# Attention and two gated layers on one core: the order of parking, reloading and forming token sums around the turn from pass one to pass two

## The chip, the cores and the metric

One core of one Trainium2 chip runs the kernel. The metric is device time in microseconds of one launch. Before the change the median of three runs is 987.12 us (986.42 to 987.84).

## The reference

The inputs are attention tensors for 4 batches of 8 heads, 512 local and 32 global positions of 64 numbers each, and the weights of two layers. After the attention there are 4 * 544 = 2176 tokens of 512 numbers (2048 local, 128 global).

```python
s_ll = where(|i - j| <= 32, scale * q_l @ k_l.T, -1e9)     # local rows see a band and the global keys
out_l = softmax([scale * q_l @ k_g.T, s_ll]) @ [v_g, v_l]
out_g = softmax(scale * q_g @ [k_g, k_l].T) @ [v_g, v_l]
x = [out_g, out_l]                                          # (2176, 512)
y = (sigmoid(x @ w_gate) * (x @ w_val)) @ w_out             # 512 -> 1536 -> 512: the gated layer
h = y @ w_in                                                # 512 -> 2048
P = a0 + a1*h + a2*h^2 + a3*h^3
Q = 1 + |b0|*|h| + |b1|*h^2
out = (P / (Q + 1e-6)) @ w_out2                             # 2048 -> 512: the rational layer
```

The change touches the gated layer and the edge to the rational one. The attention is untouched.

## The kernel before

Everything that TensorE multiplies is held as a high and a low part, and a product is three matmuls (high by high, high by low, low by high). Tokens stand in five tiles: 0 to 3 with 512 tokens each, and tile 4, the 128 global rows. `xh`/`xl` are the layer's inputs, `yh`/`yl` its outputs; they share buffers by tag (`xh0` is tile 0's high part, and so on).

**Gated layer, pass one** (line 861, six blocks of two features of 128). A block does for tile 0 `first` of both features (each 12 matmuls into `pg`, 12 into `pv`, then gate, high and low part), `first_glob` for the global rows (turned: tokens on the output's partitions), the two halves of `second` for tile 0, then `turn`, which transposes the gated global rows into `pt`, `first` of both features for tile 1, and `second_glob`. The halves of `second` for tile 1 are left pending and run in the next block, behind its first `first`. `second` adds into `acc` in SBUF (`gacc`). PSUM has two pools: ps1 with three banks (`pg`, `pv`, `pgv`, `pt`, `pty`, and `pa`, `pb`, `pc`) and ps2 with five (results of the second products).

**Weights beside it** (class `Weights`, line 450). A raw float64 weight tile is fetched and split by steps: `magnitude` (two passes on ScalarE, into a `v` tile and a `q` tile), `bits` (three on VectorE, which also asks for the raw tile three further on), `add` (GpSimd), `hi` (ScalarE), `lo` (GpSimd). For the features of pass two the gate and value tiles are also combined in four steps (`combine`, line 625) into the weights of a seven-product scheme. What is finished is stored to device memory (`keep`, line 594) and loaded back later (`pump`, line 647), in the order of `loads`, each as soon as its place in SBUF is free. `AT_ONCE` (line 458) says how many tiles of the second layer are split in each block. `Pace` (line 685) puts the steps into the instruction order: each step has a cost, `advance(dt)` is called after each piece of TensorE work, and emits steps until their summed cost has the share of the total that the time so far has of the block's 34.0.

Each engine runs its instructions in the order written here. SP's queue (SyncE) issues all DMAs, in order too: a DMA that waits holds those behind it.

**End of pass one.** The last block (features 10 and 11) makes the final sums. For tiles 0 and 1 their high and low parts are made at once in a `st` tile (three buffers, shared with the weights) and stored (lines 843 to 848): they are *parked*, since their SBUF places are needed for pass two. `final_glob` (line 804) transposes the finished global rows at the end of the block.

**Pass two** is for tiles 2 and 3. Features 0 and 1 go the plain way in the *opening* (lines 1044 to 1069). Between its pieces `combos` forms the token sums (`za` to `ze`, steps c1 to c4 for k = 0 and 1) and copies them as high and low parts (`put`) into `turned`, which lies where tiles 0 and 1 were. Features 2 to 11 go through `strassen` (line 952): seven products `g0, s2, s1, g1, s3, v1, s4` of six matmuls on three banks, with up to two pending halves of `second` put between them (after `g1` and after `s3`). At the end, line 1080, the parked tiles 0 and 1 are loaded back, and `rational` begins with tile 0.

Of the kernel before, what the change touches and what calls it, by code (L numbers as in the profile page):

```python
# [449 lines left out]
class Weights:  # L450
# [7 lines left out]
    AT_ONCE = (0, 1, 1, 1, 1, 8)  # L458
    RING2 = (4, 5, 6, 7, 0, 1, 2, 3, 8, 9, 10, 11)

    def __init__(self, tc, early, dram, ins, outs):
# [14 lines left out]
        for p, f in enumerate(range(2, NF + 1, 2)):  # L476
# [3 lines left out]
            else:  # L480
# [8 lines left out]
        self.plan = [[(0.1, step, j) for step, j in ((self.magnitude, a), (self.magnitude, b), (self.bits, a), (self.add, a),  # L489
                      (self.bits, b), (self.add, b), (self.hi, a), (self.lo, a), (self.hi, b), (self.lo, b))]]  # L490
        self.urgent, self.plan = self.plan[0], []
# [21 lines left out]
        self.loaded = 0  # L513
# [42 lines left out]
    def magnitude(self, j):  # L556
# [89 lines left out]

    def pump(self, last):

        while self.loaded < last:
# [82 lines left out]
def gated(nc, pools, only, xpool, dram, wp, ident, xh, xl):  # L732
# [48 lines left out]
    def turn(f0, t):  # L781

        ps = pools.ps1.tile([128, 512], F32, tag="p1", name=f"pt{f0}")
# [32 lines left out]
    parked = {}  # L816

    def second(f0, i, gs, half):
# [17 lines left out]
        for m in ms:  # L836
            a = acc[i][:, m]
            if f0 == 0:
                nc.vector.tensor_copy(a, ps[m])
            else:  # L840
                nc.vector.tensor_tensor(a, ps[m], a, ALU.add)  # L841
            if final:
                t = wp.stage(f"y{i}{m}") if i < 2 else None
                h, l = (yh[i][:, m], yl[i][:, m]) if i > 1 else (t[:, 0:512], t[:, 512:1024])
                nc.scalar.copy(h, a)
                (nc.vector if m % 2 else nc.gpsimd).tensor_tensor(l, a, h.bitcast(F32), ALU.subtract)
                if i < 2:
                    wp.keep((9, i, "y", m), t)
        if half == 1 and i in (1, 3):
# [8 lines left out]
    for _, step, j in wp.urgent:  # L858
        step(j)
    pending = []  # L860
    for p, f0 in enumerate(range(0, NF, G)):
        pace = Pace(wp.plan[p], 34.0)
        gs = [first(f0, 0)]
        pace.advance(2 * L)
        for half in pending:
            half()
            pace.advance(L)
        gs.append(first(f0 + 1, 0))
        pending = pair_of(f0, 0, gs)
        pace.advance(2 * L)  # L870
        t = first_glob(f0)
        pace.advance(3)
        for half in pending:
            half()
            pace.advance(L)
        gg = turn(f0, t)
        gs = [first(f0, 1)]
        pace.advance(2 * L)
# [15 lines left out]
    turned = []  # L894

    def combos():

        names = ("xh0", "xl0", "xh1", "xl1")
        t12h, t12l, t34h, t34l = (xpool.tile([128, 4, 512], F32R, tag=n, name=f"t{n}") for n in names)
        turned.extend([(t12h[:, 0:2], t12l[:, 0:2]), (t12h[:, 2:4], t12l[:, 2:4]),  # L900
                       (t34h[:, 0:2], t34l[:, 0:2]), (t34h[:, 2:4], t34l[:, 2:4])])
        part = {(r, c): (xh[2 + c][:, 2 * r : 2 * r + 2].bitcast(F32), xl[2 + c][:, 2 * r : 2 * r + 2].bitcast(F32))
                for r in range(2) for c in range(2)}

        def tile(name):
            return only.tile([128, 512], F32, tag="z", name=name, bufs=6)

        def put(i, k, src, eng):
            h, l = (t[:, k] for t in turned[i])
            nc.scalar.copy(h, src)  # L910
            eng.tensor_tensor(l, src, h.bitcast(F32), ALU.subtract)

        held = {}

        def less(dst, x, y, eng):

            for d, a, b in zip(dst, x, y):
                eng.tensor_tensor(d, a, b, ALU.subtract)
            eng.tensor_tensor(dst[0], dst[0], dst[1], ALU.add)

        def at(rc, k):
            return [t[:, k] for t in part[rc]]

        def c1(k):
            held["a", k], held["b", k] = tile(f"za{k}"), tile(f"zb{k}")
            less((held["a", k], held["b", k]), at((0, 1), k), at((0, 0), k), nc.vector)

        def c2(k):
            h, l = at((1, 1), k)
            a, b = held["a", k], held["b", k]  # L930
            nc.gpsimd.tensor_tensor(b, h, a, ALU.subtract)
            nc.gpsimd.tensor_tensor(b, b, l, ALU.add)

        def c4(k):
            h, l = at((1, 0), k)
            b = held["b", k]
            c = held["c", k] = tile(f"zc{k}")
            nc.vector.tensor_tensor(c, h, b, ALU.subtract)
            nc.vector.tensor_tensor(c, c, l, ALU.add)

        def c3(k):
            held["d", k], held["e", k] = tile(f"zd{k}"), tile(f"ze{k}")
            less((held["d", k], held["e", k]), at((1, 1), k), at((0, 1), k), nc.gpsimd)

        out = []
# [423 lines left out]
```

## Time and profile before

| what | us |
|---|---|
| median of three runs | 987.12 |
| the profiled execution | 990.42 |
| its span, first to last instruction | 988.2 |
| TensorE busy in it | 920.2 (93%) |
| VectorE busy | 743.1 (75%) |
| ScalarE busy | 581.3 (59%) |
| GpSimd busy | 570.8 (58%) |

In the profile PE is TensorE, DVE VectorE, ACT ScalarE, POOL GpSimd, and SP the queue that issues DMAs. L709 is line 709 of the kernel, and `pg<-xh,w10gv` names what an instruction writes and reads. Times are microseconds from the start of the span. "Idle before, releaser" says what an engine waited for. PEclk is the TensorE clock that was granted in a stretch, 1.00 being full. A line inside a helper stands for all of its callers, so tile names tell more. The mean granted clock of the whole span is 0.965.

### The profile page before, as it was taken

How to read it: one execution, taken by the hardware profiler on the slowest of the kernel's cores; microseconds unless marked ns; L12 is line 12 of the kernel's file. 1: busy time of each engine (PE TensorE's matmuls, PEld its weight loads, DVE VectorE, ACT ScalarE, POOL GpSimd, SP SyncE). 2: the span in 40 equal slices, each digit the busy share in tenths (PEclk: the TensorE clock that was granted, in tenths of full speed). 3: DMA queues.
4: the chain of work that ended last, by engine and by line, in shares of the span. 5: the costliest groups of instructions: out<-in, count | busy, mean ns of one | idle time of the engine just before them, and what ended most of it. 6: DMA issues, size and time to landing. Idle time of an engine off the chain costs nothing.

```text
span 988.2 us, 13773 instructions
## 1 busy us (share of the span) xinstructions
PE 920.2 (93%) x4666; PEld 756.2 (77%) x4666; DVE 743.1 (75%) x1355; ACT 581.3 (59%) x1161; POOL 570.8 (58%) x470
## 2 busy tenths in 40 slices
PE   8989999798989979768999969899999999999998
PEld 6878877687878757557888857788888888888886
DVE  6988965866768665785666655987778889888887
ACT  6979854444444443333433435777777778777773
POOL 4766755656556553564565552644456567566654
PEclk9999999999989989789999989999999999999999
DMA  8754365656656786449788774000300220020112
GB/s 301 231 193 137 88 243 193 232 194 213 224 203 216 246 305 213 181 136 404 253 293 297 265 263 179 10 1 24 126 22 0 86 86 1 1 86 1 43 54 86
DMA packets 60805, 156.24 MB, mean 158 GB/s; under 512 B 7104, under 2 KB 9152, under 8 KB 60736
## 3 DMA queue, kind: packets, MB, share of 16 engines
q1 hardware_dynamic: 60640, 155.24, 45.1%
q8 instruction: 37, 0.61, 0.3%
q14 instruction: 32, 0.26, 0.1%
q10 hardware_dynamic: 96, 0.13, 0.1%
HBM read 103.17 MB, written 52.17 MB: 157 GB/s over the span
## 4 chain that ended last, share of the span: by engine, by line
PE 69%; DVE 10%; POOL 6%; DMA 5%; ACT 5%; issue 4%; SPq 1%; POOLq 0%; DVEq 0%; ACTq 0%
PE rp L1220 6%; PE rp L1218 6%; PE rp L1219 6%; PE rp L710 5%; PE rp L711 5%; PE rp L709 5%; PE p L828 2%; PE p L829 2%; PE p L827 2%; PE pair L261 2%; PE pg L709 2%; PE pg L710 2%; PE pg L711 2%; PE pb L959 1%; PE bank L380 1%
## 5 line engine op out<-in xcount | busy, mean ns | idle before, releaser
L1135 POOL TENSOR_TENSOR v<-v,u 128x512 f32<-128x512 f32 x68 | 90.8, 1336 | 120.5 <-ACT v L1131 120.5
L1189 POOL TENSOR_TENSOR rgl<-t,rgh 128x512 fp32r<-128x512 f32 x64 | 90.0, 1406 | 40.6 <-POOL v L1135 18.9
L1143 DVE TENSOR_TENSOR t<-rp,t 128x512 f32<-128x512 f32 x68 | 46.8, 688 | 54.8 <-ACT t L1139 53.7
L1128 ACT ACTIVATE u<-rp 128x512 f32<-128x512 f32 x68 | 40.5, 596 | 73.6 <-PE rp L711 70.0
L295 POOL TENSOR_TENSOR p<-p,r 128x448 f32<-128x448 f32 x64 | 58.6, 940 | 36.3 <-DVE r L290 23.3
L1164 DVE SCALAR_TENSOR_TENSOR v<-v,u 128x512 f32<-128x512 f32 x68 | 74.7, 1099 | 0.0
L1168 DVE SCALAR_TENSOR_TENSOR t<-t,co,v 128x512 f32<-128x512 f32 x68 | 72.9, 1072 | 2.4
L280 ACT ACTIVATE p<-p,mx 128x224 f32<-128x224 f32 x128 | 60.4, 484 | 8.0 <-DVE mx L272 8.0
L841 DVE TENSOR_TENSOR gacc<-p,gacc 128x512 f32<-128x512 f32 x80 | 52.2, 684 | 14.2 <-PE p L829 14.2
L1160 DVE SCALAR_TENSOR_TENSOR v<-v,u 128x512 f32<-128x512 f32 x68 | 59.1, 869 | 1.1 <-ACT u L1156 1.1
L1131 ACT ACTIVATE v<-u,co 128x512 f32<-128x512 f32 x68 | 55.6, 817 | 2.3
L755 ACT CAST gh<-t 128x512 fp32r<-128x512 f32 x38 | 23.5, 618 | 55.2 <-DVE t L748 50.3
L1152 ACT ACTIVATE u<-v,co 128x512 f32<-128x512 f32 x68 | 49.2, 724 | 6.7 <-POOL v L1135 6.7
L1139 ACT ACTIVATE t<-rp,co 128x512 f32<-128x512 f32 x68 | 51.8, 761 | 0.5 <-POOL rgl L1189 0.5
L760 DVE TENSOR_TENSOR gl<-t,gh 128x512 fp32r<-128x512 f32 x38 | 31.9, 840 | 24.6 <-ACT gh L755 24.6
L1147 DVE SCALAR_TENSOR_TENSOR t<-t,co,rp 128x512 f32<-128x512 f32 x68 | 50.2, 738 | 0.0
L1156 ACT ACTIVATE u<-u,co 128x512 f32<-128x512 f32 x68 | 48.5, 713 | 2.3 <-DVE t L1143 2.2
L1177 ACT CAST rgh<-t 128x512 fp32r<-128x512 f32 x64 | 39.0, 610 | 15.4 <-DVE t L1168 15.4
L272 DVE CUSTOM_DVE_ANT_0 p<-pair,masks 128x224 f32<-128x224 f32 x128 | 42.2, 384 | 7.4 <-PE pair L261 6.2
L748 DVE TENSOR_TENSOR t<-pv,t 128x512 f32<-128x512 f32 x28 | 19.3, 688 | 33.9 <-PE pv L711 22.3
L1243 POOL TENSOR_TENSOR racc<-ev,racc 128x512 f32<-128x512 f32 x22 | 37.9, 1744 | 0.0
L709 PE MATMUL rp<-yh,w20in 128*128 128x512 f32 x64 | 26.1, 408 | 9.1 <-issue 9.1
(1388 smaller groups left out, 3215.9 us busy)
## 6 DMA issues: line engine op xcount, KB each, us to landing
raw1gv<-in_w_gate_val SPq DMA_DIRECT2D x24, 512.0 KB, 3.5
raw2in<-in_w_in SPq DMA_DIRECT2D x16, 512.0 KB, 4.3
raw2out<-in_w_out SPq DMA_DIRECT2D x16, 512.0 KB, 3.9
kn<-in_k_l SPq DMA_DIRECT2D x15, 448.0 KB, 5.5
raw1out<-in_w_out SPq DMA_DIRECT2D x12, 512.0 KB, 3.7
vn<-in_v_l SPq DMA_DIRECT2D x16, 256.0 KB, 4.0
out<-racc SPq DMA_DIRECT2D x16, 256.0 KB, 2.0
qn<-in_q_l SPq DMA_DIRECT2D x15, 256.0 KB, 4.7
```

The source lines that it names most:

```text
L280: nc.scalar.activation(p, p, AF.Exp, bias=s["mx", half][:, n : n + 1], scale=-1.0, accum_out=s["sm", half][:, n, 0:1])
L709: nc.tensor.matmul(ps, wh, mh[:, k], start=k == 0, stop=False)
L710: nc.tensor.matmul(ps, wh, ml[:, k], start=False, stop=False)
L711: nc.tensor.matmul(ps, wl, mh[:, k], start=False, stop=k == 3)
L1135: nc.gpsimd.tensor_tensor(s["v"], s["v"], s["u"], ALU.mult)
L1160: nc.vector.scalar_tensor_tensor(s["v"], s["v"], Q_CONST, s["u"], ALU.add, ALU.mult)
L1164: nc.vector.scalar_tensor_tensor(s["v"], s["v"], 2.0, s["u"], ALU.subtract, ALU.mult)
L1168: nc.vector.scalar_tensor_tensor(s["t1"], s["t1"], a0, s["v"], ALU.add, ALU.mult)
L1189: nc.gpsimd.tensor_tensor(s["gl"], s["t1"], s["gh"].bitcast(F32), ALU.subtract)
L1218: nc.tensor.matmul(ps, gh[:, w], wh, start=k == 0, stop=False)
L1219: nc.tensor.matmul(ps, gh[:, w], wl, start=False, stop=False)
L1220: nc.tensor.matmul(ps, gl[:, w], wh, start=False, stop=k == G - 1)
```

## The change

Seven things, all in the order of work or in buffers:

- `AT_ONCE` goes from (0, 1, 1, 1, 1, 8) to (0, 2, 2, 2, 2, 5): blocks 1 to 4 split one more tile of the second layer each, the last block three fewer. The summed cost of a middle block's steps goes from 29.3 to 32.8.
- Buffers: ring `z` (combined weights, token sums, temporaries of the products) six to five, ring `q` two to three.
- `turn` takes its bank from ps2, not from ps1.
- The parked results of tiles 0 and 1 are no longer made at once: tile 0's four go to the last two spots of the last block, tile 1's four one by one into the opening.
- In the last block and the opening, loads are asked for one by one (`allow(1)`), at spots listed by hand.
- The token sums c1, c2, c4 and c3 of k = 0 run in the last block, those of k = 1 and all `put` in the opening, in a written order; no weight is split in the opening, and the rest has a pace of 143.0 over the products (174.0 over both before). `final_glob` moves behind the opening's first `first`. In block 0 the last four of the early steps move behind its first `first`.
- The parked tile 0 is asked back in feature 11 behind the product `s1`, tile 1 behind `v1`.

```diff
-    AT_ONCE = (0, 1, 1, 1, 1, 8)
+    AT_ONCE = (0, 2, 2, 2, 2, 5)
...
-            v = self.only.tile([128, 512], U32, tag="z", name=f"v{name}", bufs=6)
+            v = self.only.tile([128, 512], U32, tag="z", name=f"v{name}", bufs=5)
...
-        q = self.early.tile([128, 512], U32, tag="q", name=f"q{name}", bufs=2)
+        q = self.early.tile([128, 512], U32, tag="q", name=f"q{name}", bufs=3)
...
+    def allow(self, n):
+        self.limit += n
+        self.pump(self.limit)
...
-        while self.loaded < last:
+        while self.loaded < min(last, len(self.loads)):
...
-        ps = pools.ps1.tile([128, 512], F32, tag="p1", name=f"pt{f0}")
+        ps = pools.ps2.tile([128, 512], F32, tag="p2", name=f"pt{f0}")
...
             if final:
-                t = wp.stage(f"y{i}{m}") if i < 2 else None
-                h, l = (yh[i][:, m], yl[i][:, m]) if i > 1 else (t[:, 0:512], t[:, 512:1024])
-                nc.scalar.copy(h, a)
-                (nc.vector if m % 2 else nc.gpsimd).tensor_tensor(l, a, h.bitcast(F32), ALU.subtract)
-                if i < 2:
+                def park(h, l, m=m):
+                    nc.scalar.copy(h, acc[i][:, m])
+                    (nc.vector if m % 2 else nc.gpsimd).tensor_tensor(l, acc[i][:, m], h.bitcast(F32), ALU.subtract)
+
+                def away(m=m, park=park):
+                    t = wp.stage(f"y{i}{m}")
+                    park(t[:, 0:512], t[:, 512:1024])
                     wp.keep((9, i, "y", m), t)
+
+                if i > 1:
+                    park(yh[i][:, m], yl[i][:, m])
+                else:
+                    parks.append(away)
...
+        extra = {}
+        if f0 + G == NF:
+            load = lambda: wp.allow(1)
+            extra = {0: [load], 1: [load], 2: [lambda: c1(0)], 3: [load], 4: [load, lambda: c2(0)], 5: [load, lambda: c4(0)],
+                     6: [load], 7: [lambda: c3(0)] + [lambda: parks.pop(0)()] * 2, 8: [lambda: parks.pop(0)()] * 2}
+        spots = iter(range(9))
+
+        def spot(dt):
+            pace.advance(dt)
+            for step in extra.get(next(spots), []):
+                step()
+
         gs = [first(f0, 0)]
-        pace.advance(2 * L)
+        if p == 0:
+            for step, j in wp.urgent[6:]:
+                step(j)
+        spot(2 * L)
...
-        if f0 + G == NF:
-            final_glob()
...
+        spot(0)
         pace.finish()
-        if f0 + 2 * G >= NF:
-            wp.pump(len(wp.loads))
...
+    def back(i):
+        yh[i] = xpool.tile([128, 4, 512], F32R, tag=f"xh{i}", name=f"yh{i}")
+        yl[i] = xpool.tile([128, 4, 512], F32R, tag=f"xl{i}", name=f"yl{i}")
+        for m in range(4):
+            t = wp.kept[9, i, "y", m]
+            nc.sync.dma_start(yh[i][:, m].bitcast(F32), t[:, 0:512])
+            nc.sync.dma_start(yl[i][:, m].bitcast(F32), t[:, 512:1024])
...
         late(2)
+        if f == NF - 1:
+            back(0)
         product(a, "g1", x[1, 0], False)
...
         product(b, "v1", turned[3], False)
+        if f == NF - 1:
+            back(1)
...
     gs = [first(0, 2)]
-    some(2)
-    pace.advance(2 * L)
-    for half in pending:
-        half()
-        some(1)
-        pace.advance(L)
-    wp.pump(len(wp.loads))
+    final_glob()
+    put(0, 0, "a", nc.vector)
+    put(1, 0, "b", nc.vector)
+    wp.allow(1)
+    pending.pop(0)()
+    put(3, 0, "c", nc.gpsimd)
+    park()
+    pending.pop(0)()
+    put(2, 0, "d", nc.vector)
+    park()
+    wp.allow(1)
     gs.append(first(1, 2))
...
-    wp.pump(len(wp.loads))
+    wp.allow(len(wp.loads))
+    pace = Pace(actions, 143.0)
```

The rest of the opening goes on in the same way: c1(1), park, c2(1), a load; behind `first(0, 3)` put, park, c4(1), a load; the two halves with two puts, c3(1) and a load; behind `first(1, 3)` the last put.

## Rows read from the trace of the kernel before

**Rows 1.** Who makes PE wait, whole span: us in total, times, longest us

```profile
PE pg L709 <- ACT t L747: 18.6, 5, 6.5
PE rp L709 <- issue: 9.1, 1, 9.1
PE pv L709 <- ACT t L747: 8.5, 2, 7.0
PE pb L959 <- ACT t L747: 7.4, 1, 7.4
...
PE pb L959 <- DVE w L974: 3.5, 2, 2.7
```

**Rows 2.** Busy time by stretch: length, then busy us (instructions) per engine, clock, DMA

```profile
core 0: us, PE busy (x) PEld busy (x) DVE busy (x) ACT busy (x) POOL busy (x), PEclk, DMA share, GB/s
124.63:159.71 35.08, 32.44 (x155) 26.65 (x154) 22.75 (x40) 18.74 (x34) 19.61 (x18) 1.00 0.65 233
159.71:331.85 172.14, 158.81 (x705) 130.47 (x704) 120.11 (x187) 78.19 (x142) 103.86 (x83) 0.94 0.60 209
331.85:381.17 49.32, 41.17 (x182) 33.17 (x180) 31.77 (x47) 22.03 (x39) 24.75 (x19) 0.90 0.77 277
381.17:423.73 42.56, 35.52 (x147) 28.81 (x145) 31.01 (x38) 13.94 (x25) 23.28 (x17) 0.88 0.48 179
423.73:463.20 39.47, 28.55 (x109) 22.29 (x108) 27.24 (x35) 15.37 (x28) 22.65 (x17) 0.88 0.74 276
583.97:600.00 16.03, 6.86 (x20) 4.34 (x20) 2.12 (x5) 4.59 (x8) 3.33 (x3) 0.68 1.03 373
...
423.74:584.50 160.76, 149.25 (x637) 121.26 (x635) 107.22 (x158) 61.19 (x109) 91.53 (x71) 0.97 0.78 275
```

**Rows 3.** PE in order of time, block 4: starts of three `pg` layers

```profile
290.17 0.39 PE L709 MATMUL pg<-xh,w18gv 128*128 128x512 f32 x1
...
301.05 0.39 PE L709 MATMUL pg<-xh,w19gv 128*128 128x512 f32 x1
...
314.97 0.48 PE L709 MATMUL pg<-xh,w18gv 128*128 128x512 f32 x1
```

**Rows 4.** ACT in order of time, block 4, in front of the late sigmoid

```profile
321.80 0.67 ACT L567 ACTIVATE q110out<-raw1out 128x512 uint32<-128x512 uint32 x1 [2.48 <-POOL v111gv L583]
...
322.63 0.61 ACT L747 ACTIVATE t<-pg 128x512 f32<-128x512 f32 x1
```

**Rows 5.** Who makes ACT wait, 331.85 to 463.20

```profile
ACT v26out L566 <- POOL st24in L613: 7.4, 1, 7.4
...
ACT sty L845 <- DMA k91y<-sty: 5.3, 2, 4.7
...
ACT sty L845 <- DMA k90y<-sty: 3.7, 2, 3.0
```

**Rows 6.** DVE and POOL in order of time: a weight's steps, gate, combining, sums

```profile
291.67 0.42 DVE L574 TENSOR_SCALAR v18out<-v18out 128x512 f32<-128x512 f32 x1
...
292.58 0.69 DVE L576 SCALAR_TENSOR_TENSOR v18out<-raw1out,v18out 128x512 uint32<-128x512 uint32 x1
...
311.52 0.42 DVE L748 TENSOR_TENSOR t_glob<-pgv,t_glob 128x256 f32<-128x256 f32 x1
...
311.68 1.29 POOL L583 TENSOR_TENSOR v111gv<-v111gv,q111gv 128x512 uint32<-128x512 uint32 x1 [1.09 <-DVE v111gv L576]
...
315.52 0.43 DVE L634 TENSOR_TENSOR v110gv<-v110gv,v110gv 128x256 f32<-128x256 f32 x1 [0.84 <-POOL v110gv L632]
...
388.99 0.69 DVE L918 TENSOR_TENSOR za<-xh,xh 128x512 f32<-128x512 f32 x1
...
404.54 1.75 DVE L938 TENSOR_TENSOR zc<-xh,zb 128x512 f32<-128x512 f32 x1
```

**Rows 7.** SP's queue at the end of pass two, and how long these loads took

```profile
574.37 0.32 SPq L658 DMA_DIRECT2D w21out<-k21out  x1
...
585.75 0.61 SPq L1085 DMA_DIRECT2D yh<-k90y  x1
...
yh<-k90y SPq DMA_DIRECT2D x4, 256.0 KB, 7.2
```

More of the change, by code (lines that the diff above doesn't have):

```diff
@@ L512, in __init__ @@
         self.two = {key: self.RING2[n % 12] for n, key in enumerate(two)}
-        self.loaded = 0
+        self.loaded = self.limit = 0
         self.places, self.free = {}, [True] * 12
@@ L814, in final_glob @@
         nc.vector.tensor_tensor(yl[GLOB], src, yh[GLOB].bitcast(F32), ALU.subtract)
-    parked = {}
+    parks = []
     def second(f0, i, gs, half):
@@ L854, in pair_of, with ztile, put, less @@
         return [lambda h=h: second(f0, i, gs, h) for h in range(2)]
-    for _, step, j in wp.urgent:
+    turned, held = [], {}
+    part = {(r, c): (xh[2 + c][:, 2 * r : 2 * r + 2].bitcast(F32), xl[2 + c][:, 2 * r : 2 * r + 2].bitcast(F32))
+            for r in range(2) for c in range(2)}
+    def ztile(name):
+        return only.tile([128, 512], F32, tag="z", name=name, bufs=5)
+    def put(i, k, x, eng):
+        if not turned:
+            t12h, t12l, t34h, t34l = (xpool.tile([128, 4, 512], F32R, tag=n, name=f"t{n}") for n in ("xh0", "xl0", "xh1", "xl1"))
+            turned.extend([(t12h[:, 0:2], t12l[:, 0:2]), (t12h[:, 2:4], t12l[:, 2:4]),
+                           (t34h[:, 0:2], t34l[:, 0:2]), (t34h[:, 2:4], t34l[:, 2:4])])
+        src = held[x, k]
+        h, l = (t[:, k] for t in turned[i])
+        nc.scalar.copy(h, src)
+        eng.tensor_tensor(l, src, h.bitcast(F32), ALU.subtract)
+    def less(dst, x, y, eng):
+        for d, a, b in zip(dst, x, y):
+            eng.tensor_tensor(d, a, b, ALU.subtract)
+        eng.tensor_tensor(dst[0], dst[0], dst[1], ALU.add)
+    def at(rc, k):
+        return [t[:, k] for t in part[rc]]
+    def c1(k):
+        held["a", k], held["b", k] = ztile(f"za{k}"), ztile(f"zb{k}")
+        less((held["a", k], held["b", k]), at((0, 1), k), at((0, 0), k), nc.vector)
+    def c2(k):
+        h, l = at((1, 1), k)
+        a, b = held["a", k], held["b", k]
+        nc.gpsimd.tensor_tensor(b, h, a, ALU.subtract)
+        nc.gpsimd.tensor_tensor(b, b, l, ALU.add)
+    def c4(k):
+        h, l = at((1, 0), k)
+        b = held["b", k]
+        c = held["c", k] = ztile(f"zc{k}")
+        nc.vector.tensor_tensor(c, h, b, ALU.subtract)
+        nc.vector.tensor_tensor(c, c, l, ALU.add)
+    def c3(k):
+        held["d", k], held["e", k] = ztile(f"zd{k}"), ztile(f"ze{k}")
+        less((held["d", k], held["e", k]), at((1, 1), k), at((0, 1), k), nc.gpsimd)
+    for step, j in wp.urgent[:6]:
         step(j)
@@ L886, in gated @@
                 wp.release((1, f0 + g, "gv", h))
+        spot(0)
         pace.finish()
-        if f0 + 2 * G >= NF:
-            wp.pump(len(wp.loads))
     actions = list(wp.plan[-1])
[L894 to L945, printed above, removed]
-        for k in range(2):
-            out += [lambda k=k: c1(k), lambda k=k: c2(k), lambda k=k: put(0, k, held["a", k], nc.vector),
-                    lambda k=k: c4(k), lambda k=k: put(1, k, held["b", k], nc.vector), lambda k=k: c3(k),
-                    lambda k=k: put(3, k, held["c", k], nc.gpsimd), lambda k=k: put(2, k, held["d", k], nc.vector)]
-        return out
@@ L970, in tile @@
         def tile(name):
-            return only.tile([128, 512], F32, tag="z", name=f"{name}{f}", bufs=6)
+            return only.tile([128, 512], F32, tag="z", name=f"{name}{f}", bufs=5)
         def add(out, ps, t):
@@ L1034, in strassen, with park @@
         return [l0, l1, l2, l3]
-    t_steps = combos()
-    pace = Pace(actions, 174.0)
-    def some(n):
-        for _ in range(n):
-            if t_steps:
-                t_steps.pop(0)()
-    gs = [first(0, 2)]
-    some(2)
-    pace.advance(2 * L)
-    for half in pending:
-        half()
-        some(1)
-        pace.advance(L)
-    wp.pump(len(wp.loads))
+    def park():
+        if parks:
+            parks.pop(0)()
+    gs = [first(0, 2)]
+    final_glob()
[9 more added lines that the diff above has]
+    wp.allow(1)
     gs.append(first(1, 2))
-    some(3)
-    pace.advance(2 * L)
+    c1(1)
+    park()
+    c2(1)
+    wp.allow(1)
     pending = pair_of(0, 2, gs)
     gs = [first(0, 3)]
-    some(3)
-    pace.advance(2 * L)
-    for half in pending:
-        half()
-        some(2)
-        pace.advance(L)
+    put(0, 1, "a", nc.vector)
+    park()
+    c4(1)
+    wp.allow(1)
+    pending.pop(0)()
+    put(1, 1, "b", nc.vector)
+    c3(1)
+    pending.pop(0)()
+    put(3, 1, "c", nc.gpsimd)
+    wp.allow(1)
     gs.append(first(1, 3))
-    some(16)
-    pace.advance(2 * L)
+    put(2, 1, "d", nc.vector)
     for f in range(G):
```

29 lines of the change are left out of this document (13 added, 16 removed).

## The prediction

> **What bounds the kernel now.** I first asked who makes TensorE (PE) wait [rows 1], because the page shows PE busy for 93% of the span and no other engine above 75%. In the two passes of the gated layer PE lost time at few places. It waited 18.6 us in five pieces before the first matmul of `pg` (6.5 us the longest), 8.5 us before `pv`, 7.4 us and 3.5 us before `pb`, and 9.1 us at the first matmul of the second layer. Most releasers are L747, the sigmoid on ScalarE (ACT) that frees a PSUM bank. The sigmoid is short, so the reader should ask what stood ahead of it in ACT's queue.
>
> Next I cut the span at the block starts [rows 2] and asked what each stretch would take without waits. From `pg` of one block to the next `pg` is 10.88 us, with 48 matmuls of 512 columns between them [rows 3], so one costs 0.2267 us at the full granted clock. From there to the next `pg` is 13.92 us; 48 matmuls of these take 10.88, which leaves 3.04 for the global rows and their transposes. A block of pass one has 150 such matmuls and these 3.04 us: 37.05 us. Against that, blocks 1 to 4 took 172.14 instead of 148.2 (23.9 lost), block 5 took 49.32 (12.3 lost), and block 0, which has 24 matmuls fewer, 35.08 instead of 31.6 (3.5 lost). The opening of pass two (144 matmuls, 32.6 us) took 42.56: 9.9 lost. The first two features of the seven-product part (54 matmuls each, 24.5 us together) took 39.47: 15.0 lost. The stretch at the reload held 20 matmuls (4.5 us) in 16.03: 11.5 lost. In sum 76 us. The granted clock of these stretches is 0.68 to 0.94 and 1.00 in block 0: a long wait is followed by matmuls at the lower level, so a loss is larger than its wait.
>
> **The change part by part.**
> *Another bank for the turned global rows, a third `q`.* In block 4 ACT stood 2.48 us before q110out until POOL had freed `q`, and only then came the sigmoid at 322.63 [rows 4], for which `pg` had to wait. With `pt` out of ps1, nine tiles instead of ten share its three banks, and the second `pg` of a half can take the bank of the global rows, read long before. The next tile that needs the sigmoid comes 2.72 us later (12 matmuls). I count these waits, with their slow matmuls, as gone: up to 23.9 us.
>
> *One more prepared weight in blocks 1 to 4.* It costs VectorE (DVE) 1.6 us (three instructions, 291.67 to 293.27) and POOL twice 1.29 us per block [rows 6], ACT three short passes, SP a fetch and a store. DVE is busy 120.1 of 172.1 us [rows 2], so 120.1 + 6.4 in some 156 is 81%: room, if nothing stands in the wrong order. One thing does. Working out the pace for 32.8 instead of 29.3 units, I find that the first two of the four combining steps move from after the global gate to before it. In block 4 DVE gated the global rows at 311.52, and ended the second combining step at 315.52 + 0.43 = 315.95, held by POOL [rows 6]. Behind it, the gate ends at about 316.4 instead of 311.94. PE transposed these rows just before the `pg` of 314.97 [rows 3], at about 314.6, and would now wait about 1.8 us. A lower bound is 0 (`q` no longer holds ACT, so the add before it comes earlier); an upper one is the old loss, 6 us a block. I take 1.8 a block: the gain is 23.9 - 7.2 = 16.7, between 0 and 23.9.
>
> *Block 5.* ACT waited 3.7 us for the parked copies' stores, since all four share three stage tiles with the weights [rows 5], and PE then waited 6.5 us [rows 1]. Afterwards the block prepares 5 weights, not 8 (three times 1.6 us less on DVE, three times 2.6 on POOL), gets the token sums c1, c2, c4, c3 for k = 0 (five DVE subtractions or additions, 0.69 us each alone, five on POOL), and parks at its two last spots. The last copy waits for the store of the first, but then 13 us pass before PE needs ACT: `first(1, 1)`'s end, the global product, `first(0, 2)`. Six reloads of 512 KB are asked for one by one, in place of four at once. The final transposes go behind `first(0, 2)`, which has no need of them. Gain 11, between 3 and 12.3.
>
> *Opening of pass two.* The stores of the second parked set held ACT 5.3 us, and a weight's v tile 7.4 us [rows 5]; PE's 7.0 and 7.4 us follow [rows 1]. Now no weight is prepared here, only three token sums, the eight copies and four parks, each between other work. DVE has some 30 instructions of 0.69 us in 33 us. Queued behind a park on ACT are the next copy and gate, on SP the next reload, needed 12 us later at the earliest. The gain is 9 in the opening (2 to 9.9). In the first two features 12 of 15: 3.5 us of waits for DVE's `w` stay in part, because there is no other product between `s3` and `v1` [rows 1].
>
> *The first parked tile earlier.* SP issued the first `yh` at 585.75, after PE's last matmul, and PE waited until it had landed, a median of 7.2 us [rows 7]. Now its eight transfers stand behind the `s1` product of feature 11, right before the request that SP issued at 574.37. That is 11 us before PE is done; 2 MB at the 373 GB/s of the reload stretch [rows 2] take 5.6. What hides them is g1, s3, v1, s4 and two halves, 48 matmuls = 10.9 us. If SP is held by a store ahead of them, up to 4 us come back, and their cost is at worst the old wait. Gain 10.5 of 11.5 (4 to 11.5).
>
> *Faster pace in the products.* 19 weights over the products, where about 16 fell there. POOL gets 7 us more on 91.5 of 160.8 [rows 2] (2.7 weights of 2.6). I take 1.5 us lost (0 to 10). Ring z of five instead of six: the slot's last reader is a feature behind, nothing.
>
> Block 0's two casts move behind its gate: 2 of 3.5 us (0 to 3.5).
>
> Sum: 2 + 16.7 + 11 + 9 + 12 + 10.5 - 1.5 = 59.7 us. The profiled execution took 990.42 us around its span of 988.2, and should come to 930.7; the median of the plain runs, 987.12, is 3.3 lower, which gives **927 us**. All lower bounds together leave about 5 us of gain (waits for `w` unchanged), all upper ones 74.
>
> **A rule against it.** A DVE addition with both inputs in SBUF took 0.69 us, and another 1.75 while POOL worked [rows 6]. The Trainium skill ("SBUF — State Buffer", section "SBUF: two separate sides") says that the port pair of DVE and GpSimd is an exclusive lock, so that the loser is blocked for a whole instruction. The trace agrees, 1.75 against 0.69. By that rule all three DVE steps of an added weight could be blocked; that is rival A.
>
> **Rivals.**
> *A: DVE's order is the new wait.* Each of the three steps pays 1.75 - 0.69 = 1.06 us more, 3.2 a block, on the critical piece before the transposes. With 1.8 us the wait is 5 us, long enough for slow matmuls, and blocks 1 to 4 give back all of 16.7. Products with POOL further behind lose 8 more. Gain 37: 950 us. For it: 1.75 us is what was measured. Against: DVE idled 30% of these blocks [rows 2], and seldom would all three steps meet POOL. Chance 0.17.
> *B: parks and reloads still bunch.* The three stage tiles stay, so ACT stands at the third park and SP at a store with the reloads behind it. Block 5 and the opening keep their losses, and the last reload half of its own: 59.7 - 25 = 35, 952 us. This is also the case in which "one at a time" doesn't do what it says. Against: block 5 has three weights fewer on the stage. Chance 0.08.
> *C: slower, by POOL in the products.* If POOL became the bound there, the gating multiply of every odd feature would come late and the half behind it would wait, as `pb` did for 7.4 us with 3 us of slow matmuls after it. Six such waits or more eat 60 us, the point from which it decides: 990 to 1000 us. It needs POOL near 95%; 98.5 of 146 us is 67%. Chance 0.05.
>
> **How the numbers follow.** Forecast 0.68, A 0.17, B 0.08, C 0.05, no measurable effect (parts that cancel) 0.02. The time is that of the forecast, 927, with 913 to 944 as its own range. The range of 912 to 954 takes in A and B and leaves out C and the far ends. About 0.2% is what a measurement can tell here: faster 0.92, same 0.03, slower 0.05.
>
> **What would show it.** Right: no `pg` wait for L747 above 2 us in blocks 1 to 4 and a new one of 1 to 2 us at the transposes of `t_glob`; block starts 38 to 39.5 us apart; no ACT cast waiting over 3 us for a store; the opening under 35 us; `yh` issued before 576 and no wait at the first matmul of the second layer above 2 us. Wrong: middle blocks over 41 us, waits for L747 in the opening, SP at the parks' stores when the products begin, or features from 4 on above 15.5 us.

## The result and the profile after

The changed kernel takes **957.46 us** (median of four runs, 957.24 to 960.25) beside 987.31 before: a ratio of 0.9705, 95% interval 0.9686 to 0.9724. It is faster, as forecast, but it gained 29.8 us instead of 60, and it stands above the range, which ended at 954. The profiled execution took 957.4 us around a span of 955.6.

First the view of busy time by stretch, with the columns of [rows 2]: block 0, blocks 1 to 4, block 5, the opening of pass two, its first two features, features 4 to 11.

```profile
125.08:156.95 31.87, 31.87 (x155) 26.82 (x153) 23.79 (x40) 18.44 (x35) 19.93 (x18) 1.00 0.71 256
156.95:329.20 172.25, 157.26 (x705) 128.54 (x704) 134.30 (x197) 83.38 (x151) 112.80 (x88) 0.96 0.65 228
329.20:367.95 38.75, 37.74 (x177) 31.13 (x176) 32.17 (x44) 17.59 (x33) 23.43 (x18) 1.00 0.76 271
367.95:401.06 33.11, 33.11 (x149) 27.42 (x148) 26.47 (x31) 13.11 (x24) 20.35 (x15) 1.00 0.63 222
401.06:431.35 30.29, 26.97 (x109) 21.11 (x108) 19.88 (x29) 11.46 (x20) 13.09 (x11) 0.94 0.85 296
431.35:552.27 120.92, 120.73 (x529) 98.72 (x528) 85.61 (x131) 50.05 (x88) 74.01 (x58) 1.00 0.86 304
```

Against [rows 2] and the forecast's terms (the products from feature 4 on ran from 463.20 to 583.97 before; "to the end" is from there to the end of the span at 988.2, and now from 552.27 to 955.6):

| stretch | before | after | gained | forecast |
|---|---|---|---|---|
| block 0 | 35.08 | 31.87 | 3.2 | 2 |
| blocks 1 to 4 | 172.14 | 172.25 | -0.1 | 16.7 |
| block 5 | 49.32 | 38.75 | 10.6 | 11 |
| opening | 42.56 | 33.11 | 9.5 | 9 |
| features 2 and 3 | 39.47 | 30.29 | 9.2 | 12 |
| features 4 to 11 | 120.8 | 120.9 | -0.1 | -1.5 |
| to the end | 404.2 | 403.3 | 0.9 | 10.5 |

Two terms are missing almost whole, 16.8 and 9.6 us; the others are right to 3 us. Who makes TensorE (PE) wait now, columns as in [rows 1]:

```profile
PE pt L789 <- DVE t_glob L752: 12.1, 4, 3.1
PE p L831 <- DVE gacc L845: 7.1, 1, 7.1
...
PE pb L979 <- DVE w L994: 3.3, 2, 2.5
...
PE pv L713 <- ACT t L751: 0.6, 1, 0.6
```

The 18.6 us of `pg` and the 7.4 us of `pb` behind the sigmoid, and the 9.1 us at the reload [rows 1], are gone. Two waits have come in their place. The first stands once in each of blocks 1 to 4, before the transposes of `t_glob`. DVE in order of time, block 4:

```profile
313.00 0.42 DVE L631 TENSOR_TENSOR v110gv<-v110gv,v110gv 128x256 f32<-128x256 f32 x1 [2.62 <-POOL w110gv L613]
314.26 0.43 DVE L634 TENSOR_TENSOR v110gv<-v110gv,v110gv 128x256 f32<-128x256 f32 x1 [0.83 <-POOL v110gv L632]
314.61 0.42 DVE L752 TENSOR_TENSOR t_glob<-pgv,t_glob 128x256 f32<-128x256 f32 x1
```

This is the order that the prediction worked out: the combining steps stand ahead of the gate L752. PE's row behind it shows 3.1 us, not 1.8:

```profile
315.08 0.51 PE L789 MATMUL pt<-ident,t_glob 128*128 128x128 f32 x2 [3.12 <-DVE t_glob L752]
```

L631 waited for the same step of GpSimd (POOL) in the kernel before, so the reckoning from 315.95 had that wait in it:

```profile
314.25 0.42 DVE L631 TENSOR_TENSOR v110gv<-v110gv,v110gv 128x256 f32<-128x256 f32 x1 [2.31 <-POOL w110gv L613]
```

What it had not is that DVE and POOL stand further behind PE now. PE's last matmul into `pgv` started at 309.24 before and at 304.75 after, so L631 started 5.0 us behind it then and 8.3 us now.

The second is the 7.1 us of `p` for `gacc`, at 573.81. It leads back to ACT, where the first `t1` of the second layer (a temporary of the rational layer, `t` in the row of L1163) waits for a store, and to SP, where that store, of the last weight split, went out behind the eight transfers of tile 1. ACT in order of time, then SP:

```profile
557.89 0.82 ACT L1155 ACTIVATE v<-u,co 128x512 f32<-128x512 f32 x1
568.35 0.78 ACT L1163 ACTIVATE t<-rp,co 128x512 f32<-128x512 f32 x1 [9.64 <-DMA k215out<-st215out]
```

```profile
551.41 0.32 SPq L597 DMA_DIRECT2D k214out<-st214out  x1
551.83 0.38 SPq L969 DMA_DIRECT2D yh<-k91y  x1
...
555.97 0.55 SPq L970 DMA_DIRECT2D yl<-k91y  x1
...
559.94 0.32 SPq L597 DMA_DIRECT2D k215out<-st215out  x1
```

The first matmul on tile 0 ran at 552.27 without a wait, so the early request did what it should. ACT then stood until 568, DVE, which waits for that `t1`, emptied no bank of `p` until 573, and PE ran out of banks in one of the first layer's last halves.

### The profile page after: what moved, and what is told of

Read it like the earlier page. It is cut to its first block, busy times and chain, and to the rows that moved or that the text cites. A ratio compares the mean times of both kernels' runs of the same rounds, so it can differ in the third digit from the quotient of the medians.

```text
span 955.6 us, 13762 instructions
## 1 busy us (share of the span) xinstructions
PE 910.9 (95%) x4666; PEld 750.5 (79%) x4666; DVE 753.0 (79%) x1355; ACT 580.9 (61%) x1161; POOL 572.5 (60%) x470
## 4 chain that ended last, share of the span: by engine, by line
PE 69%; POOL 9%; DVE 9%; issue 5%; DMA 4%; ACT 2%; SPq 1%; POOLq 0%; ACTq 0%; DVEq 0%
PE rp L1244 6%; PE rp L1242 6%; PE rp L1243 6%; PE rp L713 6%; PE rp L714 6%; PE rp L715 6%; PE pair L261 2%; PE p L833 2%; PE p L832 2%; PE p L831 2%; DMA qn<-in_q_l 2%; PE bank L380 1%; PE pg L713 1%; PE pg L714 1%; PE pg L715 1%
## 5 line engine op out<-in xcount | busy, mean ns | idle before, releaser
L1163 ACT ACTIVATE t<-rp,co 128x512 f32<-128x512 f32 x68 | 51.8, 761 | 10.1 <-DMA k215out<-st215out 9.6
L764 DVE TENSOR_TENSOR gl<-t,gh 128x512 fp32r<-128x512 f32 x38 | 34.9, 917 | 26.2 <-ACT gh L759 26.2
L261 PE MATMUL pair<-kn,qn 64*128 64x224 f32 x256 | 30.2, 368 | 1.7 <-ACT pgn L319 1.2
L362 PE MATMUL bank<-ident,p 128*128 128x128 f32 x128 | 26.6, 291 | 1.3 <-POOL p L295 1.3
```

## The experiments

Each ratio is to the kernel before in the same session, each time beside the 957.46 us of the kernel after; block lengths are from one first `pg` to the next.

### The start of the second layer

**Both tiles asked back at the end** (the kernel after without its early request).

```diff
-        if f == NF - 1:
-            back(0)
...
-        if f == NF - 1:
-            back(1)
...
     pace.finish()
+    for i in range(2):
+        back(i)
```

> The kernel after, with both parked tiles asked back only when the last weight's stores are issued, as in the kernel before. Theory (asking early saved next to nothing, since the t1 wait took the place of the reload's): TensorE waits about 9 us at the first matmul of the second layer, the t1 wait is hidden behind it, and the time is 957 to 960 us. Rival (asking early was worth its 9 us and they were lost elsewhere): 964 us or more.

961.29 us, ratio 0.9731 (0.9707 to 0.9755). PE waited 11.4 us for `yh` at the first matmul, and the `t1` behind it found its store done. So the early request, which was to give 10.5 us, gave 3.8. The time lies between the two expectations, nearer the theory.

**A pool of its own for `t1`**, and one for the stage tiles, so that `t1` no longer comes after the stage tiles' readers. No instruction changes its place.

```diff
-        return self.only.tile([128, 1024], F32R, tag="st", name="st" + name, bufs=3)
+        return self.stores.tile([128, 1024], F32R, tag="st", name="st" + name, bufs=3)
...
+        wp.stores = c.enter_context(tc.tile_pool(name="stores", bufs=1))
...
+    wp.t1 = ctx.enter_context(tc.tile_pool(name="t1", bufs=1))
     rest = ctx.enter_context(tc.tile_pool(name="rest", bufs=1))
...
-        pool = {"u": pools.t, "v": wp.early}.get(name, rest)
+        pool = {"u": pools.t, "v": wp.early, "t1": wp.t1}.get(name, rest)
```

> Nothing is reordered: the three tiles that the second layer's ACT writes first (t1) get a pool of their own that lies over the z tiles alone, so the first of them no longer has to wait for the stores that read the st tiles. Theory (what the hidden reload turned into is this wait: ACT idle 9.64 us at L1163 for the store of k215out, which SP issued at 559.94, behind the eight transfers of tile 1): no wait at the first t1, no wait of 7 us at the last matmuls of the first layer for the sums' evacuation, and 947 to 951 us against 957.5. Rival (the landing of tile 1 or the weights of the second layer set the start anyway, so another wait takes its place): 955 us or more.

949.42 us, ratio 0.9606 (0.9586 to 0.9627): 8.0 us gained by the placing of buffers alone. ACT in order of time, then PE's waits from 540 to 640:

```profile
558.53 0.82 ACT L1155 ACTIVATE v<-u,co 128x512 f32<-128x512 f32 x1
559.25 0.76 ACT L1163 ACTIVATE t<-rp,co 128x512 f32<-128x512 f32 x1
```

```profile
PE rp L1244 <- POOL rgl L1213: 4.9, 1, 4.9
```

The store still went out late (560.62); nobody waits for it now, and the wait for `gacc` is gone. The theory holds. In the kernel after, the first `t1` thus waited for a store out of a stage tile because its pool took the place of the pool that held the stage tiles; whether the two tiles overlap, no run shows.

**Tile 1 asked back last**, behind the last weight's store.

```diff
-        if f == NF - 1:
-            back(1)
...
     pace.finish()
+    back(1)
```

> Theory (queue): the second layer starts late because ScalarE's first write of t1 waits for the store of the last weight, and that store stands on SP behind the eight reloads of tile 1. With tile 1 asked back only behind that store, ScalarE's wait of 9.6 us and TensorE's of 7.1 us go, and the wait for rgl falls from 4.4 to about 2.8 us: 946 to 949 us against 957.5 of the changed kernel. Rival (backlog): VectorE and ScalarE are not done with pass two at that time and would hold TensorE anyway: 954 us or more, with the wait for gacc still over 4 us.

953.15 us, ratio 0.9646 (0.9631 to 0.966): half of it. The store was issued at 554.76 instead of 559.94, it landed 9.3 us later, and `t1` still waited 5.2 us, until 564.18. (The profile names a transfer of tile 1 as what ended this wait; the store landed 0.1 us before it.) Moving tile 1 behind the store shortens the wait; the pool takes it away.

### Features 2 and 3

**The half between `s3` and `v1`.** In these two features one half stands behind `g1` and nothing between `s3` and `v1`.

```diff
-            tail = strassen(f, queue[0:per], tail, sets)
+            tail = strassen(f, queue[0:per] if per > 1 else [lambda: None] + queue[0:per], tail, sets)
```

> The kernel after, with the one pending half of features 2 and 3 put between the products s3 and v1 instead of behind g1. Theory (the waits for w, 0.85 and 2.47 us in these features, come from a product that has nothing beside it at that place): these waits go, features 2 and 3 last 26 to 28 us together instead of 30.3, and the time is 953 to 955 us. Rival (the chain of adds is as long wherever the half stands, and the wait moves to the place that the half left): 957 us or more.

943.1 us, ratio 0.954 (0.9516 to 0.9564): 14.4 us gained, three times the theory. The stretch of features 2 and 3:

```profile
402.06:426.87 24.81, 24.80 (x110) 20.13 (x109) 19.73 (x30) 11.49 (x21) 12.21 (x11) 1.00 0.92 339
```

24.81 us is the time of its matmuls: 5.5 of the 14.4. Another 8.6 lie between the first matmul of the second layer and the end (394.7 us instead of 403.3). The empty half also moves the pace on by 2.72 us in each feature, so the weights are split earlier and SP issued the last store at 545.00, ahead of the eight transfers. The edit thus removed the `t1` wait too, which I had not seen coming.

### Blocks 1 to 4

**The buffers alone**: the kernel before with `pt` in ps2, three `q`, five `z`.

```diff
-        ps = pools.ps1.tile([128, 512], F32, tag="p1", name=f"pt{f0}")
+        ps = pools.ps2.tile([128, 512], F32, tag="p2", name=f"pt{f0}")
...
-        q = self.early.tile([128, 512], U32, tag="q", name=f"q{name}", bufs=2)
+        q = self.early.tile([128, 512], U32, tag="q", name=f"q{name}", bufs=3)
```

> The kernel before with the buffers alone: the turned global rows in ps2, a third q, five z tiles instead of six; everything else as before. Theory (the buffers do take away the pg waits, and what they give in blocks 1 to 4 is eaten again by the second weight a block): blocks 1 to 4 last 160 to 164 us together instead of 172, block 5 and the opening stay at 47 to 50 and 40 to 43 us, and the time is 975 to 980 us. Rival (the buffers give nothing by themselves): 985 us or more.

982.32 us, ratio 0.9943 (0.992 to 0.9966). Blocks 1 to 4:

```profile
160.00:321.48 161.48, 153.35 (x706) 125.17 (x705) 121.60 (x182) 74.90 (x138) 101.69 (x80) 0.99 0.64 219
```

10.7 us less than in [rows 2], as the theory said; the total is 2 us above its range, since block 5 rose to 52.6. How the 10.7 us divide between the bank and the third `q`, no run shows. PE now waits for `pv` instead of `pg`, behind another call of the same sigmoid, at the start of the block, once a block from block 2 on and up to 2.6 us. ACT in block 4 shows why:

```profile
284.60 1.14 ACT L642 CAST st9s<-v19gv 128x512 fp32r<-128x512 f32 x2 [3.12 <-DVE v19gv L634]
285.64 0.59 ACT L747 ACTIVATE t<-pg 128x512 f32<-128x512 f32 x1
```

The casts of the combined weights hold ACT. They did so in the kernel before as well. There PE, held by its `pg` wait, began block 4 only at 290.17 [rows 3], and did not have to wait for this sigmoid. ACT in the kernel before, then its waits in blocks 1 to 4, which I did not read:

```profile
286.52 1.14 ACT L642 CAST st9s<-v19gv 128x512 fp32r<-128x512 f32 x2 [3.17 <-DVE v19gv L634]
287.56 0.59 ACT L747 ACTIVATE t<-pg 128x512 f32<-128x512 f32 x1
```

```profile
ACT st3s L642 <- DVE v13gv L634: 5.6, 1, 5.6
ACT st4s L642 <- DVE v14gv L634: 5.2, 1, 5.2
...
ACT st7s L642 <- DVE v17gv L634: 3.2, 1, 3.2
```

**One weight a block** in the kernel after, eight in block 5.

```diff
-    AT_ONCE = (0, 2, 2, 2, 2, 5)
+    AT_ONCE = (0, 1, 1, 1, 1, 8)
```

> The changed kernel with the weights per block as before (1 in blocks 1 to 4, 8 in the last, 20 left for pass two). Theory (order): at the old pace the combining steps fall behind the global gate again, blocks 1 to 4 take 151 to 156 us; the last block pays 1 to 5 us for its three weights, pass two up to 2: 937 to 945 us. Rival (load of the weight itself, whatever the order): the same blocks gain as much, but then holding the steps back with the weight kept in place gains nothing.

958.9 us, ratio 0.9702 (0.9685 to 0.9718). Blocks 1 to 4 took 162.25 us, more than the theory's 151 to 156, since PE waits 7.0 us for `pv` behind the casts there; so the second weight costs 10.0. Block 5 (44.54) and the opening (37.38) lose 10.1: the trade is even.

**The turned rows back in ps1** in the kernel after.

```diff
-        ps = pools.ps2.tile([128, 512], F32, tag="p2", name=f"pt{f0}")
+        ps = pools.ps1.tile([128, 512], F32, tag="p1", name=f"pt{f0}")
```

> The changed kernel with the turned global rows back in the three-bank pool. Theory (order): the bank did matter, but its wait is now partly hidden by the one at the transposes: waits of pg for the sigmoid come back in blocks 1 to 4 at 1 to 3 us each, 960 to 972 us. Rival: the third q buffer alone had cured the old wait, the bank is worth nothing: within 1 us of 957.5.

958.36 us, ratio 0.9699 (0.9685 to 0.9714). Not to be told from 957.46, as the rival had it. PE waits 12.0 us for `t_glob` in blocks 1 to 4 and not for `pg` or `pv`: the bank is not what comes last in this order.

**The combining steps behind the global gate.** A step of that name ends the emission at the spot ahead of `first_glob` and runs at the next.

```diff
+            if step.__name__ == hold:
+                return
...
         pending = pair_of(f0, 0, gs)
-        spot(2 * L)
+        spot(2 * L, "combine")
         t = first_glob(f0)
```

> Theory (order): blocks 1 to 4 gained nothing because VectorE's two first combining steps stand ahead of the gate of the global rows. With the combining steps held until that gate is written, the four waits of 3.1 us at the transposes and the slow matmuls behind them go: blocks 1 to 4 in 152 to 156 us instead of 172, 938 to 942 us in all. Rival (load): with one more weight a block VectorE and GpSimd are too busy, the waits come back at other places: blocks 1 to 4 over 164 us, 949 us or more.

956.79 us, ratio 0.9682 (0.9667 to 0.9696). The wait for `t_glob` is gone, and PE waits up to twice a block for `pv` behind the sigmoid, up to 2.3 us; blocks 1 to 4 took 168.43. The casts hold ACT 5.8 and 3.2 us. My theory of one misplaced step fell. The edit holds the steps in block 5 too, and that block took 42.0 us instead of 38.75: of the 3.8 us gained in blocks 1 to 4, 3.3 are lost again there.

**The same, with the casts one weight later in the list.**

```diff
-                            out += [(0.6, self.combine, self.order[i][1], n) for n in range(4)]
+                            out += [(0.6, self.combine, self.order[i][1], n) for n in range(2)]
+                            wait = [(0.6, self.combine, self.order[i][1], n) for n in range(2, 4)]
```

> The kernel after, with the four combine steps of a block kept out of the spot ahead of the global gate, and their last two steps (those with the ACT casts) each one item later in the list. Theory (in blocks 1 to 4 the chain of combines holds whatever stands behind it in order on its engine: DVE's t_glob in the kernel after, ACT's sigmoid behind the casts L642 where the steps came later): with the casts apart from the sums they depend on, neither the wait for t_glob nor the one of pv for ACT is over 1 us, blocks 1 to 4 last 38 to 39.5 us each and the time is 941 to 946 us. Rival (the engines beside TensorE have too much to do in these blocks, wherever it stands): the waits move again, blocks of 41 to 43 us, 951 us or more.

957.3 us, ratio 0.9685 (0.9664 to 0.9706): the rival. `pv` hardly waits now; once a block the half waits 2.5 to 3.1 us for `gh`, the high part of the second feature, whose gate stands on DVE behind a weight's three steps.

**Without the additions.** The sums that the second pass reads are left out; casts and stores stay.

```diff
-            nc.vector.tensor_tensor(a1, a0, a1, ALU.add)
-            nc.gpsimd.tensor_tensor(a0, g0, a0, ALU.subtract)
...
-            nc.vector.tensor_tensor(g0, a1, g0, ALU.subtract)
...
-            nc.vector.tensor_tensor(g1, g1, g0, ALU.subtract)
```

> The kernel after without the four additions and subtractions of the combining steps (three on DVE, one on POOL, two features a block; their casts and stores stay), so the sums that the second pass reads are left out. Theory (in blocks 1 to 4 it is the chain DVE, POOL, DVE, DVE, with what stands behind it in order, that TensorE waits for): no wait for t_glob over 1 us, blocks 1 to 4 of 37.3 to 39 us, 935 to 943 us against 957.5. Rival (the sheer work of the second weight on DVE and POOL): blocks of 40.5 us or more, 950 us or more.

935.16 us, ratio 0.9461 (0.9439 to 0.9483). Blocks 1 to 4:

```profile
156.25:306.52 150.27, 149.82 (x705) 124.58 (x704) 132.40 (x169) 84.14 (x154) 111.03 (x79) 1.00 0.75 259
```

PE waits 0.45 us in 150, at the full clock, while DVE is busy 132.4 us, 88%. The 22.0 us that the kernel after loses here are 14.5 of waits (172.25 - 157.26 against 0.45) and 7.4 of slower matmuls (157.26 against 149.82). A DVE that is busy 88% thus holds PE up 0.45 us in all, once the chain is out of its queue. Its busy time is a poor measure of its work, too: 27 additions of 0.42 us went, 11.4 us, and it fell by 1.9.

**The additions' work without their chain.** The three DVE additions keep place and size, but read the token tile and write a spare one; POOL's subtraction and the sums are left out.

```diff
-            nc.vector.tensor_tensor(a1, a0, a1, ALU.add)
+            nc.vector.tensor_tensor(self.spare, a, b, ALU.add)
```

> The kernel after with the work of the combining additions but without their chain: the three DVE additions of a feature stand at their old places and keep their size (128x256), but read the token tile xh2 and write one spare tile, so that they wait for nothing; the POOL subtraction is left out, and so are the sums that the second pass reads. Theory (blocks 1 to 4 wait for the order of the chain, not for DVE's time): blocks of 37.2 to 38.7 us and no wait for t_glob over 1 us, 934 to 940 us, beside 935.2 without any additions. Rival (DVE's load: these additions fill it up): blocks of 40.5 us or more, 948 us or more.

945.54 us, ratio 0.9567 (0.9545 to 0.9588), between theory and rival. Blocks 1 to 4, then the additions (min, median, max in ns):

```profile
156.86:315.76 158.90, 152.65 (x705) 125.55 (x704) 143.25 (x193) 83.81 (x153) 109.73 (x79) 0.99 0.70 244
```

```profile
L632 DVE TENSOR_TENSOR spare<-xh x30: 409/1281/1523, 145.0 to 318.0; 128x256 f32<-128x256 f32 x30
```

13.4 of the 22.0 us go with the chain; 8.6 stay with the work. The split is rough: these additions took 1.28 us and the chained ones 0.42, so the work weighs more here, but POOL's subtractions (nine of 0.73 us) are gone with the chain.

**The chain on DVE alone**, behind the gate, with the half of features 2 and 3 moved (943.1 us is its base, and that of the runs below).

```diff
-            nc.gpsimd.tensor_tensor(a0, g0, a0, ALU.subtract)
+            nc.vector.tensor_tensor(a0, g0, a0, ALU.subtract)
```

> The half of features 2 and 3 between s3 and v1 (943.1 us), the combining steps behind t_glob's gate as in the second run of this study, and their one POOL step done by DVE, so that the five additions of a feature stand on one engine. Theory (what costs the time is the crossing between DVE and POOL inside the chain, with ACT's casts behind it): the casts no longer hold ACT over 2.5 us, the waits of pv for ACT fall below 1 us, blocks 1 to 4 of 38 to 40 us, 925 to 934 us. Rival (the chain starts behind the weight's last step on POOL wherever it is, and ACT stands that long): waits of 1 to 2.5 us for ACT stay, 41 us or more a block, 937 us or more.

**939.76 us**, ratio 0.9514 (0.9495 to 0.9532): the fastest whole kernel of the study. Two waits of `pv` a block are left, 1.9 and 0.8 us, in blocks of 42 us (39.7 the first). The cast still holds ACT 5.5 us. That is what the rival said: crossing between engines is not the whole of it, and ACT stands as long as the chain starts behind the weight's last step. Blocks 1 to 4 took 165.70 us, 6.6 less than in its base, and block 5 took 41.7, 2.9 more. Holding the steps in blocks 1 to 4 alone was not run.

**The chain on POOL alone**, without and with the casts one weight later.

```diff
-            nc.vector.tensor_tensor(a1, a0, a1, ALU.add)
+            nc.gpsimd.tensor_tensor(a1, a0, a1, ALU.add)
```

> The half of features 2 and 3 between s3 and v1 (943.1 us), and all four additions of a combining step on POOL, which also does the weight's last step that they must wait for; the order as in the kernel after. Theory (DVE, which gates what TensorE reads, must not stand in the chain): no wait of the transposes for t_glob, but the casts L642 hold ACT until POOL is done, 6 to 8 us, and the casts and sigmoids behind them are late: blocks of 39.5 to 42 us, 930 to 940 us. Rival (POOL becomes the bound of blocks 1 to 4 with 3 us more a block): blocks of 43 us or more, 945 us or more.

> As the run before it, with the two casts of a feature (combining steps 2 and 3) one weight later in the list. Theory (neither DVE nor ACT stands behind the chain then): no wait of TensorE over 1 us in blocks 1 to 4, blocks of 37.5 to 39 us, 920 to 928 us. Rival (POOL becomes the bound with 3 us more a block, and gl or the weights come late): blocks of 41 us or more, 937 us or more.

948.11 us, ratio 0.959 (0.9575 to 0.9604), and 942.09, 0.953 (0.9514 to 0.9546). In the first, `t_glob` waits no more, the casts hold ACT 7.1 and 4.0 us, and `pv` waits for that, 2.9 us: 5.0 us slower than its base. Blocks 1 to 4 took 172.66 us there, as in the base (172.29); the loss lies behind them. In the second they hold it 3.7 and 3.0, and `pv` still waits 2.3: 1.0 faster. Both times lie in the rivals' ranges, but that POOL was the bound is not shown: it was busy 78% and 84% of these blocks.

**Other orders.** The DVE chain with casts one weight later gave 942.43 us, 0.9539 (0.9518 to 0.9561), and with casts half a weight later 940.4, 0.9518 (0.9497 to 0.954). Each had a wait of 1.4 to 3 us a block again, for `gh` in the first, mostly for `pv` in the second, as the rivals had it:

> The kernel of 939.8 us (half between s3 and v1, combining steps behind t_glob's gate, their additions on DVE alone), with the two casts of a feature one weight later. Theory (the one wait left a block, 1.9 us of pv for the sigmoid, stands behind a cast that held ACT 5.5 us for the chain): no cast waits over 2.5 us, blocks 1 to 4 of 37.5 to 39.5 us, 923 to 931 us. Rival (DVE is too full in these blocks, so that another gate is late instead): waits of 1.5 us or more at another place of each block, 41 us or more, 936 us or more.

> As the run before it, but the two casts stand only behind the next weight's first steps (magnitude, bits, addition) and ahead of its last ones. Theory (a cast needs only some 3 us more to find its sums ready): as the run before it, 923 to 933 us, and the third stage tile is free earlier. Rival (as there): 936 us or more.

Two orders with POOL's step in the chain were worse than their base of 943.1: all four steps later, at the spot that the casts have in the run half a weight later, 950.66, 0.9619 (0.9593 to 0.9645), and the held steps with later casts, with a weight's three DVE steps held as well, 948.65, 0.9601 (0.958 to 0.9622).

> The same place for the half of features 2 and 3 (943.1 us), and the four combining steps of a feature emitted one weight later than their sums are ready, with no other change to the order: the first of them then has no POOL step to wait for. Theory (t_glob is late because DVE stands 2.6 us in front of the first combining step for POOL): the t_glob wait falls below 1 us, blocks 1 to 4 of 38 to 40 us, 925 to 934 us. Rival (the order is only shifted, and another gate stands behind the combining steps): blocks of 41 us or more, 938 us or more.

> The half of features 2 and 3 between s3 and v1 (which gave 943.1 us), and the combining steps with their casts later, and also the three DVE steps of a weight kept out of the spot ahead of the second feature's gate in blocks 1 to 4, where DVE's order made TensorE wait 2.5 us a block for gh. Theory (one wait a block is left, and it is a matter of DVE's order): blocks 1 to 4 of 37.5 to 39.5 us, 921 to 930 us. Rival (DVE is the bound of these blocks, so a wait taken away at one place comes back at the next): blocks of 41 us or more, 936 us or more.

Nine other orders of the chain, and in nearly every block of each a wait of 1 to 4 us. An order that has none was not found.

## Why the prediction was wrong

**Blocks 1 to 4, the step "I count these waits, with their slow matmuls, as gone: up to 23.9 us".** Measured, the buffers give 10.7. The `pg` waits went, but under them another was hidden: the casts of the combined weights held ACT 3.2 us ahead of the sigmoid at the start of a block as well, and a PE that comes earlier waits for it, up to 2.6 us. [Rows 5] shows ACT's waits from 331.85 on; had I asked the same view for blocks 1 to 4, the waits of the casts, 3.2 to 5.6 us, would have stood in it.

**The step "the gain is 23.9 - 7.2", 1.8 us a block for the second weight.** The place was right, DVE's gate behind two combining steps. The size was 3.1 us, and slower matmuls came on top. The rows from which I reckoned [rows 6] stand in the kernel before, with one weight less a block. With the second weight, L631 starts 3.2 us later behind PE's last `pgv` matmul; PE itself comes 1.6 us later to the transposes. All in all the second weight costs 10.0, not 7.2, and 10.7 - 10.0 is about the nothing that was measured. Part of this is a sum that was too small: I priced a weight on DVE at 1.6 us by its three shortest rows, and DVE's busy time rose by 14.2 us where I had 6.4. The three steps of a second weight in the kernel after, which POOL worked beside from 285.64 on:

```profile
285.28 0.42 DVE L574 TENSOR_SCALAR v21out<-v21out 128x512 f32<-128x512 f32 x1
285.74 1.49 DVE L575 TENSOR_SCALAR v21out<-v21out 128x512 uint32<-128x512 uint32 x1
287.26 1.65 DVE L576 SCALAR_TENSOR_TENSOR v21out<-raw2out,v21out 128x512 uint32<-128x512 uint32 x1
```

**The reload, the step "What hides them is g1, s3, v1, s4 and two halves".** True of the transfers, and PE did not wait for them. I looked only at SP ahead of them ("if SP is held by a store ahead of them"). Behind the next eight stood a store for which ACT waited 9.64 us; the kernel before hid that wait under the reload's own 9.1 (there the store went out at 583.04, and the first `t1` started at 599.98 without a wait). The pool run shows the term's true size: the same early request is then worth 961.3 - 949.4 = 11.9, if asking late leaves no other wait.

**Features 2 and 3: 9.2 for 12.** The waits for `w` and slow matmuls are worth 5.5 us, where I kept 3.

**Right by their own steps:** block 5 (10.6 for 11), the opening (9.5 for 9), block 0, and the pace of the products, where POOL was busy 74.0 of 120.9 us and delayed nothing. The forecast's list named 1 to 2 us at the transposes (it was 3.1) and blocks over 41 us as the mark of an error: they were 41 to 45.

**Rival A** had the mechanism of blocks 1 to 4 (DVE's order as the new wait, slow matmuls, all of the 16.7 given back) and much of its reason: it put a weight's three steps at 1.6 + 3.2 = 4.8 us, and DVE's busy time rose by 3.55 us a block. Its loss in the products did not come, and its sum is 59.7 - 16.7 - 8 = 35, not 37. I called it unlikely because DVE idled 30% of these blocks. The run without additions shows that idle share says nothing here: 88% busy, 0.45 us of waits.

The rest is the reference point: the profiled execution of before stood 3.3 us above its median, and I took the same for the kernel after, where it stood 0.1 below.

## What to carry to other kernels

Before counting a wait as gone, read the waits of the engine that released it, in that very stretch: an instruction of that queue that waits for another engine, and that nobody notices yet, can take the old wait's place. When a wait is hidden rather than shortened, list what was hidden under it (here a pool's first tile waiting for stores) and what is queued behind the transfers that moved. Instructions that pass a value back and forth between engines hold up what stands behind them in each queue: here they cost PE 22.0 us in four blocks though no engine was full. Leaving them out, with casts and stores kept, measures that in one run.

## What the runs showed of the hardware

A DVE addition of 128x256 took 0.42 us in the combining chain, where it runs after POOL has finished, and a median of 1.28 us (up to 1.52) in the run without the chain, when it was free to run at any time. The Trainium skill ("SBUF — State Buffer", section "SBUF: two separate sides") says that a DVE instruction with two SBUF inputs and a GpSimd instruction that reads SBUF lock each other out of their common ports for a whole instruction. These times agree with that, though no run took POOL's work away to show it. In this kernel a DVE instruction that is freed from a wait can thus become three times as long.
